# A second gate copy on the sync queue, ReLUs on two engines, and a newly searched order in a fused attention and gated FFN kernel

## The chip, the cores and the metric

The kernel runs on one core of a Trainium2 chip. The metric is the device time of one execution in microseconds (us), lower is better. The core has five engines with queues of their own: TensorE (PE, with its weight loads as PEld), VectorE (DVE), ScalarE (ACT), GpSimd (POOL) and SyncE (SP, which here only starts transfers). Transfers that SP, ACT or POOL start run on 16 DMA engines.

## The reference

Forgetting attention over 8 batches of 8 heads, 576 positions and head width 64, and then a gated FFN with a convolution of three taps along the sequence. All inputs and the output are float32.

```python
q, k, v, f: (8, 8, 576, 64), f: (8, 8, 576)
scores = q @ k.T / 8
cum = cumsum(log(clip(f, 1e-4, 1)), axis=-1)
scores = where(causal, -1e9, scores + cum[:, None] - cum[None, :])
x = softmax(scores) @ v                      # heads side by side: (8, 576, 512)
h = maximum(x @ w_in, 0)                     # (8, 576, 1024)
conv = sum over k of conv_w[k] * h shifted by k - 1 along the sequence
out = (h * sigmoid(conv)) @ w_out            # (8, 576, 512)
```

## The kernel before, in words

The work is cut into named tasks. A task has the engines that it may run on, the tasks that must stand before it, and rooms that it takes and gives back: four PSUM tiles `ps` of 1024 float32 columns, six tiles `pp` for probabilities, two buffers `hg` for the FFN's hidden units and so on. The string `ORDER` is a list of all tasks; `Plan.play` runs through it once and issues each task's instructions, with the engine behind the `@` where a task has a choice. So `ORDER` sets the order on each engine, and which buffer a task gets. The engines then run their own queues and wait for one another by semaphores.

A half batch (`hb`, 16 of them) is four heads. For it:

- `q{hb}.0` and `q{hb}.1` load q and k by a transposing transfer that leaves the high and low half of each float32 in alternate rows (L229). `cl` scales these rows and sets constant ones (L235). The even rows then get the decay: `rw` writes three rows from a small DRAM image (L251, L252); from half batch 8 on, without `cl`, `fi` writes 60 rows of zeros and four rows (L243, L245). Four buffers `qk` are used in turn. For half batches 0 and 1, `ld` loads plainly, `tp` turns on PE (L215) and `cl` copies out of PSUM (L221, L223).
- `v` loads values (L258) and `va` casts them (L266, L268).
- `st`, `sd` and `so` are scores on PE (L359): the tails of 64 positions, the diagonal blocks of two heads, and the off-diagonal blocks of one head. `et`, `ed` and `eo` are their exponentials on ACT (L379, L400, L417). For half batches 0 to 7 a matmul adds the causal mask (L367); from 8 on POOL masks behind the exponential (`mt`, `md`, L382, L403).
- `pv` multiplies with the values (L441, L445), `n` normalizes on DVE (L453, L455), and `t` with `tx` turns the result on PE and copies it (L462, L472). For half batches 10 to 15 `tx` is a transposing transfer from SP instead (L467).

For a batch `b`, with eight slices `ff` of 128 hidden units: `f{b}.{ff}` is the first matmul (L481), `r` the ReLU with a factor of one half (L491), `c` and `d` the two steps of the convolution on DVE (L496, L498), `a` a tanh on ACT (L501), `g` the gate on DVE (L505), `k` a copy of the last 64 positions so that two batches share one block (L510), `o` the second matmul (L516), `e` the copy from PSUM and `s` the store. The last batch's `o`, `e` and `s` go by chunks of 128 positions and by `ff` (L526, L532).

The decay at the start: f lies on 128 partitions, all 64 heads twice, loaded by two transfers of ACT's queue. `dca` clips it (L567), `dcl` takes the logarithm (L312), `dcs` is the running sum (L316), `dck` splits it into bfloat16 parts (L319, L320), `ki` writes the image. `cw` and `cwt` turn the convolution's weights on PE and make ratios of them (L341, L344 to L351). `wi` and `wo` load the weights, `wic` and `woc` cast them (L551, L559).

SP issues nearly all transfers in one queue, and an issue waits there for what its data need, with everything behind it.

## Time and profile before

| what | value |
|---|---|
| median of three runs | 255.22 us (253.63 to 257.57) |
| profiled execution: time | 254.81 us |
| profiled execution: span | 253.1 us |
| busy PE / DVE / ACT / POOL | 230.6 / 215.3 / 209.3 / 60.2 us |
| transfers | 49.98 MB, mean 197 GB/s |

The span runs from the first to the last instruction; the time has 1.7 us more around it. Busy time is the union of an engine's instructions. A group in the profile is named by line, engine, operation, and output and input, with its count, its busy time, the mean of one instruction, and the idle time ahead of it with what ended that. Chain rows give a start, a length and an engine with its tile and line; they follow back what released each step from the end of the kernel.

### The profile page before, as it was taken

How to read it: one execution, taken by the hardware profiler on the slowest of the kernel's cores; microseconds unless marked ns; L12 is line 12 of the kernel's file. 1: busy time of each engine (PE TensorE's matmuls, PEld its weight loads, DVE VectorE, ACT ScalarE, POOL GpSimd, SP SyncE). 2: the span in 40 equal slices, each digit the busy share in tenths (PEclk: the TensorE clock that was granted, in tenths of full speed). 3: DMA queues.
4: the chain of work that ended last, by engine and by line, in shares of the span. 5: the costliest groups of instructions: out<-in, count | busy, mean ns of one | idle time of the engine just before them, and what ended most of it. 6: DMA issues, size and time to landing. Idle time of an engine off the chain costs nothing.

```text
span 253.1 us, 6392 instructions
## 1 busy us (share of the span) xinstructions
PE 230.6 (91%) x2618; PEld 146.2 (58%) x2618; DVE 215.3 (85%) x322; ACT 209.3 (83%) x285; POOL 60.2 (24%) x92
## 2 busy tenths in 40 slices
PE   0799989688999999999999999999959999999992
PEld 0687765357555766766565665665645755644440
DVE  5756064999999999999999989999949999999970
ACT  2746948799899989999899999999957999679661
POOL 8302011101407102221731145402414150000100
PEclk9979999999999999999999999999989999999999
DMA  7993999999999989999999999999998954045046
GB/s 161 326 276 76 218 223 168 233 220 243 223 247 209 218 187 222 237 233 222 194 245 206 242 194 255 213 185 275 230 179 174 198 163 88 7 128 201 6 166 208
DMA packets 121013, 49.98 MB, mean 197 GB/s; under 512 B 111010, under 2 KB 111010, under 8 KB 120984
## 3 DMA queue, kind: packets, MB, share of 16 engines
q1 hardware_dynamic: 120434, 48.41, 88.9%
q0 software_dynamic: 304, 0.73, 0.9%
q10 hardware_dynamic: 246, 0.44, 0.6%
q8 instruction: 20, 0.33, 0.5%
q14 instruction: 9, 0.07, 0.1%
HBM read 21.11 MB, written 10.17 MB: 124 GB/s over the span
## 4 chain that ended last, share of the span: by engine, by line
PE 57%; DVE 15%; DMA 13%; ACT 6%; issue 4%; SPq 2%; POOL 0%; ACTq 0%; DVEq 0%
PE ps L516 21%; PE ps L481 15%; PE ps L359 9%; PE ps L441 6%; DMA qk<-in_q_dram 5%; DVE u L496 4%; DVE u L498 3%; ACT pp L417 3%; DMA qk<-blank 3%; DVE hg L505 2%; DMA qk<-in_k_dram 2%; DMA u<-in_f_dram 2%; PE ps L445 2%; DVE xm L455 1%; PE ps L367 1%
## 5 line engine op out<-in xcount | busy, mean ns | idle before, releaser
L481 PE MATMUL ps<-xt,w_in_f 128*128 128x512 f16 (+1 forms) x512 | 69.3, 286 | 2.1 <-POOL w_in_f L559 1.6
L359 PE MATMUL ps<-qk 128*128 128x64 bf16 (+2 forms) x576 | 63.9, 242 | 4.5 <-DMA qk<-blank 2.6
L417 ACT ACTIVATE pp<-ps 128x1024 f16<-128x1024 f32 x64 | 64.0, 1042 | 2.8 <-PE ps L364 1.9
L516 PE MATMUL ps<-w_out_f,hg 128*128 128x512 f16 x256 | 59.3, 379 | 0.0
L498 DVE SCALAR_TENSOR_TENSOR u<-ht,cwt,u 128x576 f32<-128x576 f16 x64 | 56.2, 895 | 0.7
L496 DVE SCALAR_TENSOR_TENSOR u<-ht,cwt 128x576 f32<-128x576 f16 x64 | 54.0, 853 | 0.8 <-ACT ht L491 0.7
L501 ACT ACTIVATE hg<-u,cw 128x576 f16<-128x576 f32 x64 | 48.8, 788 | 5.5 <-DVE u L498 5.2
L359 PEld LDWEIGHTS <-qk 128*128 128x128 bf16 x576 | 39.8, 99 | 22.9 <-issue 4.6
L481 PEld LDWEIGHTS <-w_in_f 128*128 128x128 f16 x512 | 34.3, 98 | 31.3 <-POOL w_in_f L559 1.9
L505 DVE SCALAR_TENSOR_TENSOR hg<-hg,ht 128x576 f16<-128x576 f16 x64 | 50.2, 810 | 0.5 <-ACT hg L501 0.5
L491 ACT ACTIVATE ht<-ps 128x576 f16<-128x576 f32 x64 | 41.6, 674 | 6.3 <-DVE hg L505 2.6
L516 PEld LDWEIGHTS <-hg 128*128 128x128 f16 x256 | 23.8, 98 | 25.8 <-DVE hg L505 0.8
L403 POOL TENSOR_SCALAR_AFFINE_SELECT pp<-pd 128x1024 f16<-128x1024 f32 x16 | 20.4, 1282 | 55.8 <-ACT pd L400 55.8
L441 PE MATMUL ps<-va,pp 128*128 128x65 f16 x640 | 25.0, 196 | 1.4 <-ACT pp L417 1.2
L455 DVE TENSOR_TENSOR xm<-ps,rc 128x896 f16<-128x896 f32 (+1 forms) x32 | 24.2, 758 | 1.1
L441 PEld LDWEIGHTS <-pp 128*128 128x128 f16 x640 | 23.0, 99 | 3.7 <-ACT pp L417 1.1
L400 ACT ACTIVATE pd<-ps 128x1024 f32<-128x1024 f32 x16 | 16.4, 1041 | 5.0 <-PE ps L359 4.2
L400 ACT ACTIVATE pp<-ps 128x1024 f16<-128x1024 f32 x16 | 16.1, 1040 | 4.1 <-PE ps L359 4.1
L510 POOL COPY tl<-hg 128x512 f16<-128x512 f16 (+1 forms) x9 | 5.9, 669 | 45.6 <-DVE hg L505 45.6
L453 DVE RECIPROCAL rc<-ps 128x14 f32<-128x14 f32 (+1 forms) x32 | 6.6, 206 | 11.5 <-PE ps L441 7.7
L367 PE MATMUL ps<-mask,ident 128*128 128x512 bf16 (+1 forms) x40 | 14.7, 370 | 0.7 <-ACT pp L417 0.6
L266 POOL CAST va<-vf 128x1024 f16<-128x1024 f32 x7 | 8.5, 1226 | 25.9 <-PE ps L359 11.6
(91 smaller groups left out, 202.8 us busy)
## 6 DMA issues: line engine op xcount, KB each, us to landing
vf<-in_v_dram SPq DMA_DIRECT2D x32, 256.0 KB, 4.3
out_dram<-ob SPq DMA_DIRECT2D x14, 512.0 KB, 2.8
qk<-blank SPq DMA_DIRECT2D x8, 540.0 KB
ob<-in_moe_w_in_dram SPq DMA_DIRECT2D x4, 512.0 KB
ob<-in_moe_w_out_dram SPq DMA_DIRECT2D x4, 512.0 KB, 4.6
vf<-in_v_dram SPq DMA_DIRECT2D x8, 128.0 KB, 2.9
out_dram<-ob SPq DMA_DIRECT2D x4, 256.0 KB
out_dram<-ob SPq DMA_DIRECT2D x7, 128.0 KB, 2.8
```

The lines of the kernel that those rows point to most:

```text
L359: nc.tensor.matmul(o, tk[:, h * S + k0:h * S + k0 + 128], tq[:, h * S + q0:h * S + q0 + n], start=first, stop=last and not by_matmul(hb, h))
L400: nc.scalar.activation(o, ps_of(f"sd{i}").rearrange("p (s c) -> p s c", s=2), AF.Exp, scale=SCALE)
L417: nc.scalar.activation(pair(i)[:, s, 512:1536], ps_of(f"so{i}.{s}"), AF.Exp, scale=SCALE)
L441: nc.tensor.matmul(ps[:, c:c + D + 1], block(hb, h, m, n), va[:, h, m, 0:D + 1], start=(m == 0), stop=(m == n))
L455: nc.vector.tensor_tensor(x.rearrange("p (j h d) -> p j h d", j=a, d=D), got[:, :, :, 0:D], r.unsqueeze(3).broadcast_to((128, a, g, D)), o ...
L481: nc.tensor.matmul(ps[:, c:c + n], w_in_f16[:, cc, 128 * ff:128 * (ff + 1)], xt[:, cc // 2, x:x + n], start=(cc == 0), stop=(cc == NCC - 1))
L491: nc.scalar.activation(ht_of(b, ff)[:, 1:1 + S], ps_of(f"f{b}.{ff}")[:, 0:S], AF.Relu, scale=0.5)
L496: nc.vector.scalar_tensor_tensor(u, ht[:, 0:S], cwt[:, ff, 0:1], ht[:, 1:1 + S], op0=ALU.mult, op1=ALU.add)
L498: nc.vector.scalar_tensor_tensor(u, ht[:, 2:2 + S], cwt[:, ff, 1:2], u, op0=ALU.mult, op1=ALU.add)
L501: nc.scalar.activation(hg_of(b, ff), u_t[slot[f"c{b}.{ff}", "u"]], AF.Tanh, scale=cw[:, ff, 1:2])
L505: nc.vector.scalar_tensor_tensor(hv, hv, 1.0, ht_of(b, ff)[:, 1:1 + S], op0=ALU.add, op1=ALU.mult)
L516: nc.tensor.matmul(ps[:, 512 * (c % 2):512 * (c % 2 + 1)], w, w_out_f16[:, ff, :], start=(ff == 0), stop=(ff == NFF - 1))
```

## The change

Six things change in the code, and the order of all tasks with them.

The second copy of f is issued by SP instead of ACT. The load of the exponential's table is a task `tb` that must stand behind `dcl`, and each exponential behind `tb`. A ReLU may run on ACT or on DVE; on DVE it is a multiplication and a maximum in one instruction. A weight cast may also run on DVE. The last batch's chunk 1 is copied out in two halves of 256 columns, one on ACT and one on DVE, and stored by two transfers, of SP and of ACT. `ORDER` is another list. In it nine of the 64 ReLUs are on DVE (r0.0, r0.2, r0.6, r2.1, r3.3, r4.2, r4.5, r4.6, r6.2), DVE has four `tx` copies instead of seven and five output copies instead of four beside the half chunk, and `wic1` is on POOL, `woc3` on DVE. Chunk 1 of the last batch is the last one now instead of chunk 3. The clamp cl1.1.1, the last that rw1 needs, is on ACT behind scores of half batch 0 instead of on DVE.

On PE, st2, so5.0, so4.0 and so5.1 stood among f0.0 to f0.4; now so5.0, so4.0, so4.1, sd7, so7.1, sd6, st3 and so6.0 do. On SP, rw3 stood behind q5.1, v1.0 and v1.2, now ahead of q5.1. Around half batch 14, PE now has f4.7, so24.1, sd26, sd27, o3.2, so26.1, f5.0, so27.0, o3.3, f5.1, f5.2, f5.3, so25.0, f5.4, so27.1, so26.0, o4.0, st13, sd28, with n11.1 on DVE while f4.7 runs. Behind pv13.1 it has f5.5, f5.6, f5.7, so28.1, o3.4, f6.0, f6.1, o4.2, sd31. Behind the last gate g7.7 the list has 22 matmuls of the last batch where it had 18.

```diff
 ORDER = """
-ld0 ld0.1.1 ld0.0.0 ld0.0.1 ld0.1.0 tp0.0.0 tp0.0.1 ld1 dca dcl tp0.1.0 tp0.1.1 cl0.0.0@ACT dcs dck ki@POOL ld1.0.0
+dca dcl ld0 v0.0 ld0.0.0 ld1 tb cw cwt ld0.0.1 ld0.1.0 tp0.0.0 ld0.1.1 dcs tp0.0.1 tp0.1.0 v0.4 ld1.0.0 dck ld1.0.1
...
     nc.scalar.dma_start(fsb[0:BH], f.rearrange("b h s -> (b h) s"))
-    nc.scalar.dma_start(fsb[BH:128], f.rearrange("b h s -> (b h) s"))
+    nc.sync.dma_start(fsb[BH:128], f.rearrange("b h s -> (b h) s"))
     nc.scalar.preload_act_table(AF.Ln)
     nc.scalar.dma_start(cwrow, moe_conv_w)
...
     def decay_log():
         nc.scalar.activation(fsb, fsb, AF.Ln)
-        nc.scalar.preload_act_table(AF.Exp)
...
-    def relu(b, ff):
-        nc.scalar.activation(ht_of(b, ff)[:, 1:1 + S], ps_of(f"f{b}.{ff}")[:, 0:S], AF.Relu, scale=0.5)
+    def relu(b, ff, e):
+        o, i = ht_of(b, ff)[:, 1:1 + S], ps_of(f"f{b}.{ff}")[:, 0:S]
+        if e == "ACT":
+            nc.scalar.activation(o, i, AF.Relu, scale=0.5)
+        else:
+            nc.vector.tensor_scalar(o, i, 0.5, 0.0, op0=ALU.mult, op1=ALU.max)
...
+    def evac_half(b, c, x):
+        o = ob_t[slot[f"e{b}.{c & ~1}", "ob"]][:, c % 2, 256 * x:256 * (x + 1)]
+        i = ps_of(f"o{b}.{c & ~1}.0")[:, 512 * (c % 2) + 256 * x:512 * (c % 2) + 256 * (x + 1)]
+        (nc.vector.tensor_copy if x else nc.scalar.copy)(o, i)
+
+    def store_half(b, c, x):
+        r = b * S + 128 * c
+        (nc.scalar if x else nc.sync).dma_start(outf[r:r + 128, 256 * x:256 * (x + 1)],
+                                                ob_t[slot[f"e{b}.{c & ~1}", "ob"]][:, c % 2, 256 * x:256 * (x + 1)])
...
+    add("tb", "ACT", [], lambda: nc.scalar.preload_act_table(AF.Exp), behind=["dcl"])
...
-            add(f"{w}c{j}", "POOL/ACT", [f"{w}{j}"], lambda e, w=w, j=j: stage_cast(w, j, e), give=[("ob", f"{w}{j}")])
+            add(f"{w}c{j}", "POOL/ACT/DVE", [f"{w}{j}"], lambda e, w=w, j=j: stage_cast(w, j, e), give=[("ob", f"{w}{j}")])
...
-            add(f"r{b}.{ff}", "ACT", [f"f{b}.{ff}"], lambda b=b, ff=ff: relu(b, ff), take=["ht"], give=[("ps", f"f{b}.{ff}")])
+            add(f"r{b}.{ff}", "ACT/DVE", [f"f{b}.{ff}"], lambda e, b=b, ff=ff: relu(b, ff, e), take=["ht"], give=[("ps", f"f{b}.{ff}")])
...
         if last:
             for c in range(NKB):
+                if c == 1:
+                    for x in range(2):
+                        add(f"e{b}.{c}.{x}", ("ACT", "DVE")[x], [f"o{b}.{c}.{NFF - 1}"], lambda b=b, c=c, x=x: evac_half(b, c, x),
+                            behind=[f"e{b}.{c - 1}"])
+                        add(f"s{b}.{c}.{x}", ("SP", "ACT")[x], [f"e{b}.{c}.{x}"], lambda b=b, c=c, x=x: store_half(b, c, x))
+                    continue
```

Three places of the new order follow, each as it stands on an engine's queue before and then after the change. Line numbers of the changed kernel are its own.

DVE where the first FFN begins, before. `xt` copies are tx0 and tx1, the clamps of `qk1` and `qk3` belong to half batches 5 and 3, and `u0` from `ht0` is the first convolution.

```order
L472 COPY xt0_117<-ps3_136 128x1152
L472 COPY xt0_117<-ps2_135 128x1152
L235 TENSOR_SCALAR qk1_86<-qk1_86,lim_76 128x2304
L496 SCALAR_TENSOR_TENSOR u0_124<-ht0_119,cwt_72 128x576
L235 TENSOR_SCALAR qk3_88<-qk3_88,lim_76 128x2304
L498 SCALAR_TENSOR_TENSOR u0_124<-ht0_119,cwt_72,u0_124 128x576
```

The same place after; `ht0` from `ps2` is a ReLU on DVE.

```order
L238 TENSOR_SCALAR qk3_88<-qk3_88,lim_76 128x2304
L474 COPY xt0_117<-ps1_134 128x1152
L497 TENSOR_SCALAR ht0_119<-ps2_135 128x576
L502 SCALAR_TENSOR_TENSOR u0_124<-ht0_119,cwt_72 128x576
L238 TENSOR_SCALAR qk1_86<-qk1_86,lim_76 128x2304
L504 SCALAR_TENSOR_TENSOR u0_124<-ht0_119,cwt_72,u0_124 128x576
```

The first ReLU and the first convolution moved ahead of the clamp of half batch 5, and one xt copy left DVE.

SP where half batch 14 is loaded into `qk2`, before: the transfers of `xm` are tx10 and tx11, the blank and image rows are fi14.

```order
L229 DMA_TRANSPOSE qk2_87<-in_k_dram 128x2304
L258 DMA vf0_89<-in_v_dram 128x8x64 x2
L467 DMA_TRANSPOSE xt1_118<-xm1_110 128x9x128
L537 DMA out_0_dram<-ob0_130 128x2x512
L467 DMA_TRANSPOSE xt1_118<-xm0_109 128x9x128
L258 DMA vf0_89<-in_v_dram 64x8x64
L537 DMA out_0_dram<-ob2_132 128x2x512
L229 DMA_TRANSPOSE qk2_87<-in_q_dram 128x2304
L258 DMA vf1_90<-in_v_dram 128x8x64 x2
L243 DMA qk2_87<-blank_66 60x4x1152
L245 DMA qk2_87<-image_65 4x2x2304
```

The same place after.

```order
L469 DMA_TRANSPOSE xt1_118<-xm1_110 128x9x128
L232 DMA_TRANSPOSE qk2_87<-in_q_dram 128x2304
L469 DMA_TRANSPOSE xt1_118<-xm0_109 128x9x128
L232 DMA_TRANSPOSE qk2_87<-in_k_dram 128x2304
L261 DMA vf1_90<-in_v_dram 128x8x64 x2
L246 DMA qk2_87<-blank_66 60x4x1152
L248 DMA qk2_87<-image_65 4x2x2304
```

The two stores and the tail load of v that stood between tx10 and the second load of half batch 14 are gone from there.

SP where half batch 15 is filled, in `qk3`, before: the two transfers of `xm` are tx12 and tx13.

```order
L229 DMA_TRANSPOSE qk3_88<-in_q_dram 128x2304
L229 DMA_TRANSPOSE qk3_88<-in_k_dram 128x2304
L258 DMA vf1_90<-in_v_dram 128x8x64 x2
L243 DMA qk3_88<-blank_66 60x4x1152
L245 DMA qk3_88<-image_65 4x2x2304
L467 DMA_TRANSPOSE xt0_117<-xm1_110 128x9x128
L467 DMA_TRANSPOSE xt0_117<-xm0_109 128x9x128
```

The same place after.

```order
L232 DMA_TRANSPOSE qk3_88<-in_q_dram 128x2304
L261 DMA vf0_89<-in_v_dram 128x8x64
L469 DMA_TRANSPOSE xt0_117<-xm0_109 128x9x128
L553 DMA out_0_dram<-ob1_131 128x2x512
L261 DMA vf0_89<-in_v_dram 64x8x64
L469 DMA_TRANSPOSE xt0_117<-xm1_110 128x9x128
L246 DMA qk3_88<-blank_66 60x4x1152
L248 DMA qk3_88<-image_65 4x2x2304
```

Both transfers of `xm`, a store and a load of v now stand ahead of the fill.

110 lines of the change are left out of this document (57 added, 53 removed).

## The prediction

> **What bounds the kernel now.** I read the page first, then the busy time by stretches of the span, then the chain of waits, the waits of each engine, and the timeline at the places that the change touches. The page shows three engines near their limit.
>
> ```profile
> span 253.1 us, 6392 instructions
> PE 230.6 (91%) x2618; PEld 146.2 (58%) x2618; DVE 215.3 (85%) x322; ACT 209.3 (83%) x285; POOL 60.2 (24%) x92
> ```
>
> The next view cuts the span into stretches. In each row stand the length, then the busy time of PE, PEld, DVE, ACT and POOL, the granted TensorE clock, the DMA share and GB/s.
>
> ```profile
> 0.00:14.10 14.10, 5.93 (x63) 5.45 (x64) 9.27 (x26) 6.56 (x6) 7.20 (x34) 0.97 0.95 248
> 14.10:39.20 25.10, 24.02 (x336) 18.37 (x334) 12.39 (x22) 16.19 (x19) 2.59 (x3) 0.95 0.96 188
> 39.20:60.00 20.80, 16.46 (x190) 10.18 (x190) 16.82 (x22) 18.83 (x27) 3.10 (x4) 1.00 1.03 220
> 60.00:80.00 20.00, 19.03 (x214) 11.97 (x214) 19.23 (x28) 18.66 (x26) 5.89 (x5) 1.00 1.06 225
> 80.00:180.00 100.00, 99.38 (x1224) 63.71 (x1223) 96.99 (x139) 95.37 (x132) 29.77 (x35) 1.00 1.09 222
> 180.00:190.00 10.00, 7.36 (x99) 5.29 (x97) 6.55 (x11) 6.95 (x10) 2.74 (x3) 0.87 1.11 200
> 190.00:240.00 50.00, 50.00 (x467) 27.76 (x465) 48.95 (x71) 40.96 (x61) 8.33 (x8) 0.99 0.47 121
> 240.00:253.10 13.10, 8.40 (x39) 3.48 (x37) 5.06 (x10) 5.81 (x10) 0.59 (x3) 0.97 0.51 181
> ```
>
> PE is idle for 253.1 - 230.6 = 22.5 us: 8.2 before the first score matmul at 14.1, 1.1 to 39.2, 4.3 to 60, 1.0 to 80, 0.6 in the next hundred, 2.6 in the stretch 180:190, none to 240, and 4.7 at the end. The matmuls that remain are as dense as they get: in the last chain piece below, 64 of them take 13.83 us, 216 ns each. The change leaves the number of matmuls alone, so on PE only these 22.5 us can be won. DVE is next. From 80 to 180 it is busy 97.0%, from 190 to 240 97.9%.
>
> ```profile
> 234.58 13.83 PE ps L516 x64
> 248.43 0.58 ACT ob L526
> ```
>
> For DVE I take the stretch in which the FFN runs, from the first convolution to the last gate; the two rows behind it, of the timeline, are its two ends.
>
> ```profile
> 43.30:244.30 201.00, 192.46 (x2170) 118.41 (x2167) 192.06 (x274) 180.24 (x252) 48.80 (x51) 0.99 0.92 196
> ```
>
> ```profile
> 42.51 0.88 DVE L235 TENSOR_SCALAR qk<-qk,lim 128x2304 uint16<-128x2304 uint16 x1 [3.40 <-DMA qk<-in_q_dram]
> ...
> 242.86 1.42 DVE L505 SCALAR_TENSOR_TENSOR hg<-hg,ht 128x576 f16<-128x576 f16 x2
> ```
>
> The clamp at 42.51 (cl5.0) waits for its transposing load, and the first convolution stands behind it. The last gate ends at 244.28, and 8.8 us later the span ends. Between 42.51 and 244.28 lie 201.8 us, of which DVE works 192.06 + 0.8 = 192.9 and is idle 8.9. So PE and DVE are both within 5% of full there: what helps one alone is soon stopped by the other.
>
> **The change, part by part.**
>
> *Second half of f on SP, cwt ahead of the sum.* The decay chain starts the kernel. These are pieces of the chain, a wait of SP's queue, and rows of the timeline.
>
> ```profile
> 1.39 5.69 DMA u<-in_f_dram
> ...
> 8.39 1.37 DVE u L316
> ...
> 11.07 1.49 DVE qk L223
> ```
>
> ```profile
> SPq L258 <- DMA u<-in_f_dram: 2.2, 1, 2.2
> ```
>
> ```profile
> 5.44 0.37 SPq L258 DMA_DIRECT2D vf<-in_v_dram  x1
> ...
> 11.04 0.66 PE L341 MATMUL ps<-one,pd 3*128 3x3 f32 x8 [0.59 <-ACT qk L221]
> ...
> 13.85 0.17 DVE L344 COPY cw<-ps 128x24 f32<-128x24 f32 x1
> ...
> 15.00 0.16 DVE L351 TENSOR_TENSOR cwt<-cw,cwt 128x8 f32<-128x8 f32 x1
> ```
>
> The second copy is issued at 1.39 and lands at 7.08; SP's load at 5.44 was released by the first, so that one had landed. Issued first on SP, the second should land by 5.44 too: 1.6 us earlier. But DVE now makes the conv ratios before the running sum, and PE their transposes before all else. The conv row takes the place in ACT's queue that the second f copy leaves, so I put its landing between 5.4 and 7.1; then come 0.66 us on PE and 15.16 - 13.85 = 1.3 on DVE, and the sum starts between 7.4 and 9.1 instead of 8.39. What is won on f is mostly spent again; ratios no longer lie between the clamps later. Bounds for the first FFN matmul: 2.0 earlier to 1.3 later (when rw1's last clamp, now on ACT behind scores, comes late by that). I take **-0.6**. The exp table as a task of its own has one answer: it stands behind dcl on ACT as before, 0. SP's loads of q and k stand behind one more issue and v0.0; they are covered, since their clamps wait for the decay rows until 11.07.
>
> *More scores ahead of f0.4.* PE's waits have one for the third weight cast.
>
> ```profile
> PE ps L481 <- POOL w_in_f L559: 1.6, 1, 1.6
> ```
>
> In the changed order two more diagonal and two more off-diagonal blocks of scores stand between f0.0 and f0.4, and rw3, on which they rest, is issued before q5.1 instead of behind it. Bounds -1.6 to 0. I take **-1.0**, nearer to the row than to 0, because the added scores need rw3's landing, which this trace can't show.
>
> *The stall at 184.* The chain shows it, with the length of a score block and of an f in its first two rows; the rows behind are of the timeline.
>
> ```profile
> 130.71 0.44 PE ps L359 x4
> 131.14 0.98 PE ps L481 x8
> ...
> 173.98 5.88 DMA qk<-in_q_dram
> ...
> 179.87 6.46 DMA qk<-blank
> ...
> 186.43 1.04 PE ps L359 x12
> ```
>
> ```profile
> 170.82 1.66 SPq L467 DMA_TRANSPOSE xt<-xm  x1
> ...
> 174.15 3.10 PE L481 MATMUL ps<-xt,w_in_f 128*128 128x512 f16 x24
> ...
> 193.84 0.95 SPq L243 DMA_DIRECT2D qk<-blank  x1
> ...
> 200.31 1.06 PE L359 MATMUL ps<-qk 128*128 128x128 bf16 x16
> ```
>
> fi14 is issued 9.0 us after tx11, because q14.0 stands behind tx11, a v load that waits for GpSimd, and a store. Behind the change only q14.1 and two loads stand between: 1.5 + 5.9 = 7.4 us, landing 6.5 later, 13.9 us after tx11. In the changed order PE has, from n11.1's end, the rest of f4.7, four score blocks and o3.2, 0.2 + 1.8 + 1.7 = 3.7 us, until f5.0, and then 10.2 until sd28 (five f at 0.98, o3.3 and o4.0 at 8 x 0.216 = 1.73, four score blocks at 0.44, a tail): it arrives at 13.9. The wait of 2.6 goes. So does the slow clock behind it: 0.13 of 10 us in the row 180:190 and up to 0.01 of 50 in the next, 1.3 to 1.8 us. Bounds -4.4 to 0, taken **-4.1** on PE. The Trainium skill, page "TensorE: Matmul & The Clock Gate", section "Part 1: The HAM clock gate (the "warmup" mystery)", says that the clock falls after an idle window of about 3.4 us. By that rule a wait of 2.6 us would leave the clock alone, and this term would be -2.6. The trace disagrees, since the clock fell behind this wait; so I keep the larger value.
>
> *fi15 behind tx12 and tx13.* Before, fi15 went out at 193.84 and was used at 200.31, 6.5 us later, without a wait. Now both transposes of xm, a store and a v load stand ahead of it on SP, and tx13 waits for n13.1. PE has 2.9 + 0.4 + 1.7 = 5.1 us of work between pv13.1 and f6.0, and 3.7 more to sd31. tx12 and tx13 take 1.3 to 3 us each to issue, with 1.2 between; landing within 3.3 us, as tx11 to f5.0 above. That makes 0 to 3.6 us of new waiting, **+1.5** taken.
>
> *Work that changes engines.* Rows of the groups, by form:
>
> ```profile
> L491 ACT ACTIVATE ht<-ps 128x576 f16<-128x576 f32 x64 | 41.6, 674 | 6.3 <-DVE hg L505 2.6 <-PE ps L481 2.5 <-ACT hg L501 0.8
> ...
> L472 DVE COPY xt<-ps 128x1152 f16<-128x1152 f16 x7 | 5.1, 751 | 1.0 <-PE ps L464 1.0
> ...
> L268 POOL CAST va<-vf 64x256 f16<-64x256 f32 x6 | 3.1, 522 | 16.3 <-DMA vf<-in_v_dram 16.3
> ...
> L522 DVE COPY ob<-ps 128x1024 f32<-128x1024 f32 x2 | 2.4, 1219 | 0.3 <-PE ps L516 0.3
> ...
> L526 DVE COPY ob<-ps 128x512 f32<-128x512 f32 x1 | 0.7, 692 | 0.8 <-PE ps L516 0.8
> ```
>
> A ReLU on DVE has no row. From PSUM, 512 columns take 692 ns and 1024 take 1219, 1.03 ns a column; 576 take 0.76 us (bounds 0.69 and 0.85, the latter the convolution's mean in the page). Nine move. ACT loses 9 x 0.674 = 6.1 us; it was not the last to come free, so that wins nothing by itself. On DVE, within the stretch from cl5.0 to the last gate: 8 x 0.76 = +6.1 (r0.0 and c0.0 now run ahead of cl5.0, in the 3.40 us for which DVE waited there: -0.8 for c0.0); two xt copies fewer, -1.5; one v cast fewer and one weight cast more, 0; two output copies of 1024 more and one of 512 fewer, +1.8. Less 0.6 for the overlap of neighbours (two convolutions show 1.54, not 1.62): **+5.0 us of DVE work**, 197.9 in all. The other weight cast moves from ACT to GpSimd, at 33 us, where both wait for data: 0.
>
> *Last chunk in halves.* A copy of 256 columns takes 0.43 us on DVE by the same slope, against 0.58 for the last copy on ACT: **-0.15**. The stores carry the same bytes; I count nothing there (bounds -0.5 to +0.3, two issues beside each other on two queues).
>
> **The sum.** PE's side: -0.6 - 1.0 - 4.1 + 1.5 - 0.2 = -4.4, a span of 248.7. DVE's side: start of cl5.0 at 42.5 - 0.6 = 41.9; 197.9 of work; idle 2.0, that is 99% busy, between the 97.9% of 190:240 and full, because the stall (10 - 6.55 of the row 180:190) goes; the last gate then ends at 241.8. Behind it stand 22 matmuls instead of 18, +0.9, less 0.15: 8.8 + 0.7 = 9.5 to the end. That is a span of 251.3. The later side decides: 251.3, or 1.8 less than before. The profiled execution took 254.81, 1.7 beside its span; so **253.0**. The median of the three runs is 255.22, 0.4 over the profiled one, and I leave that difference out.
>
> **The rivals.** *PE's side decides* (0.25): DVE's added work fits into waits that its row counts as busy. For it speaks that ACT gets 6 us freer, so that PSUM buffers come back sooner. It gives 248.7 + 1.7 = 250.4, and 248.5 where the start wins its full 2.0 and the w_in wait its 1.6.
>
> *DVE runs no fuller than from 80 to 180* (0.2): at 97%, 197.9 takes 204.0, the last gate ends at 245.9, and the time is 255.4 + 1.7 = 257.1, slower than before. It decides from a DVE share under 98.1%, where 41.9 + 201.7 + 9.5 is the old span. Against it: from 80 to 180 PE was busy 99.4%, so DVE's 3% there were mostly waits for PE, and from 190 to 240 it stood at 97.9%, next to that point. For it stands a stretched convolution, 1.70 us instead of 0.82, while a GpSimd mask of 1.10 runs:
>
> ```profile
> 171.91 1.10 POOL L403 TENSOR_SCALAR_AFFINE_SELECT pp<-pd 128x1024 f16<-128x1024 f32 x1 [8.86 <-ACT pd L400]
> 171.92 1.70 DVE L498 SCALAR_TENSOR_TENSOR u<-ht,cwt,u 128x576 f32<-128x576 f16 x1
> ```
>
> Three more v tails move to GpSimd, 3 x 0.52 us, worth 0.8 each us beside such a convolution: +1.3. The Trainium skill, "GPSIMD Engine Reference", section "1. Specifications", states this as a rule against moving work there: the SBUF interfaces are shared, and DVE instructions with two SBUF inputs contend. The two rows above bear it out.
>
> *The wait moves to fi15* (0.1): 3.6 us, and the clock falls as above, 1.5: PE's side is 248.7 + 3.6 = 252.3, 254.0 in time.
>
> *The new order does nothing* (0.05): every wait reappears, 253.1 + 1.7 = 254.8. The forecast itself has 0.4; its own range is 251 to 255.
>
> **How the numbers follow.** The range 247.5 to 257.5 reaches from PE's side with its best terms to the DVE rival; outside it I leave the full sum of all gains and the case of several late costs, 2 in 10. Two per cent of 255.2 is 5.1 us, about what a measurement of this kernel can tell from no change. Faster than 250.1: most of PE's side and a little of the forecast, 0.27. Slower than 260.3: the tail of the DVE rival and of fi15, 0.10. Within: 0.63.
>
> **What would show it.** f landing by 5.5 and the running sum between 7.4 and 9.1; no PE wait for a qk<-blank transfer near 184 and the clock at 1.00 there; PE waiting at most 3 us for xt or qk<-blank just before the last scores; DVE at 98 to 99% between its first convolution and the last gate, with nine ReLUs near 0.76; the end 9 to 10 us behind the last gate. The forecast is wrong if PE's idle time falls by over 6 us with DVE under 97%, or if DVE's own work grows by clearly more than 5.

## The result, and the profile after

The changed kernel takes 255.94 us in the median of 20 executions (254.53 to 261.17); the kernel before, run beside it, 256.35 in the median of 20 (252.62 to 259.49). The ratio of the two, taken over the executions that lie within 1.5% of the fastest of their kernel, is 1.0103 with a 95% interval of 1.0071 to 1.0134: about one per cent slower, where 0.7% faster had been forecast, and less than the two per cent from which a kernel is called faster or slower here. The two medians are nearly equal all the same, because only 10 of the 20 executions of the kernel before are as quick as those that the ratio is taken from, and 15 of the 20 of the changed one. The profiled execution of the changed kernel took 255.84 us, its span 254.1; the forecast was 253.0 and the profiled one of before 254.81. So the gain of 1.8 us did not come; the time is inside the range of 247.5 to 257.5.

The page's busy times, and the stretches of the prediction for the changed kernel (columns as there):

```profile
span 254.1 us, 6397 instructions
...
PE 229.6 (90%) x2618; PEld 144.8 (57%) x2618; DVE 218.6 (86%) x328; ACT 205.5 (81%) x276; POOL 65.3 (26%) x96
```

```profile
0.00:14.10 14.10, 6.08 (x58) 5.33 (x59) 10.63 (x32) 4.56 (x4) 7.40 (x34) 1.00 0.89 247
14.10:39.20 25.10, 23.62 (x349) 18.22 (x347) 10.87 (x15) 18.99 (x22) 5.08 (x5) 1.00 1.15 202
39.20:60.00 20.80, 17.66 (x207) 11.15 (x206) 18.39 (x24) 19.39 (x28) 2.51 (x3) 1.00 1.02 213
60.00:80.00 20.00, 18.10 (x213) 11.68 (x211) 19.56 (x29) 18.14 (x25) 7.77 (x10) 1.00 1.02 225
80.00:180.00 100.00, 98.17 (x1184) 62.40 (x1183) 97.62 (x137) 91.66 (x123) 28.88 (x30) 1.00 1.07 218
180.00:190.00 10.00, 8.76 (x156) 6.43 (x155) 8.98 (x13) 8.63 (x13) 4.43 (x6) 1.00 1.08 257
190.00:240.00 50.00, 46.91 (x422) 25.19 (x423) 45.66 (x71) 38.16 (x57) 6.38 (x9) 0.97 0.43 115
240.00:254.10 14.10, 10.28 (x48) 4.38 (x45) 6.90 (x13) 5.91 (x10) 2.82 (x2) 1.00 0.48 168
```

PE's idle time is the first number less the second. It was 8.2, 1.1, 4.3, 1.0, 0.6, 2.6, 0 and 4.7 us; now it is 8.0, 1.5, 3.1, 1.9, 1.8, 1.2, 3.1 and 3.8, in all 24.5 instead of 22.5. What the stretches 39.2:60 and 180:190 and the two ends gained (3.6 together) is lost again at 14.1:39.2, at 60 to 180 and above all at 190:240, where before there was no idle time (5.6 together). Two shorter stretches of it, and waits that are new, four of PE and one of ACT behind which PE waits in its turn:

```profile
190.00:200.00 10.00, 6.91 (x67) 3.68 (x68) 9.90 (x18) 7.55 (x12) 0.38 (x2) 1.00 1.05 240
200.00:210.00 10.00, 10.00 (x116) 5.85 (x114) 6.02 (x9) 6.75 (x10) 1.86 (x3) 0.83 0.04 9
```

```profile
PE ps L483 <- DMA xt<-xm: 4.2, 2, 3.1
...
PE ps L464 <- DVE xm L457: 1.4, 2, 1.2
...
ACT ob L528 <- DMA out_dram<-ob: 1.4, 1, 1.4
...
PE ps L443 <- ACT ob L528: 1.2, 1, 1.2
...
PE ps L483 <- DVE xm L457: 1.0, 1, 1.0
```

The timeline of PE and of SP's queue shows the place. `L469` are tx12 and tx13, `L553` the store s4.0, `L261` value loads, and the 12 matmuls of `L483` f6.0 and f6.1:

```profile
186.35 2.40 PE L443 MATMUL ps<-va,pp 128*128 128x65 f16 x72 [1.24 <-ACT ob L528]
...
195.47 0.65 PE L483 MATMUL ps<-xt,w_in_f 128*128 128x512 f16 x4
199.22 2.18 PE L483 MATMUL ps<-xt,w_in_f 128*128 128x512 f16 x12 [3.09 <-DMA xt<-xm]
201.21 3.04 PE L522 MATMUL ps<-w_out_f,hg 128*128 128x512 f16 x8
```

```profile
185.64 4.21 SPq L232 DMA_TRANSPOSE qk<-in_q_dram  x1
189.89 0.58 SPq L261 DMA_DIRECT2D vf<-in_v_dram  x1
190.87 2.14 SPq L469 DMA_TRANSPOSE xt<-xm  x1
193.11 0.52 SPq L553 DMA_DIRECT2D out_dram<-ob  x1
193.72 0.69 SPq L261 DMA_DIRECT2D vf<-in_v_dram  x1
194.51 1.73 SPq L469 DMA_TRANSPOSE xt<-xm  x1
```

tx12 waits behind q15.0 and v7.2, tx13 behind s4.0 and v7.4. PE has the first four matmuls of f6.0 from tx12, then waits 3.1 us for tx13. Behind that the clock is 0.83 in the mean of 200:210, so eight matmuls of 512 columns take 3.04 us instead of the 1.89 that eight of the same line take at 205, and DVE is busy for only 6.0 of these 10 us. The wait for fi14 that stood at 184 is gone, and the clock in 180:190 is 1.00.

### The profile page after: what moved, and what is told of

Read it like the earlier page. It is cut to its first block, busy times and chain, and to the rows that moved or that the text cites. A ratio compares the mean times of both kernels' runs of the same rounds, so it can differ in the third digit from the quotient of the medians.

```text
span 254.1 us, 6397 instructions
## 1 busy us (share of the span) xinstructions
PE 229.6 (90%) x2618; PEld 144.8 (57%) x2618; DVE 218.6 (86%) x328; ACT 205.5 (81%) x276; POOL 65.3 (26%) x96
## 2 busy tenths in 40 slices
DMA packets 121157, 49.98 MB, mean 197 GB/s; under 512 B 111026, under 2 KB 111282, under 8 KB 121128
## 4 chain that ended last, share of the span: by engine, by line
PE 59%; DMA 19%; SPq 7%; ACT 7%; DVE 5%; issue 2%; ACTq 0%
PE ps L522 19%; PE ps L483 18%; PE ps L361 10%; DMA qk<-in_k_dram 7%; PE ps L443 5%; SPq L232 4%; DMA hg<-in_q_dram 3%; ACT pp L419 3%; DMA qk<-blank 3%; PE ps L369 2%; DMA out_dram<-ob 2%; DMA xt<-xm 2%; DMA qk<-image 2%; PE ps L447 2%; DVE u L502 1%
## 5 line engine op out<-in xcount | busy, mean ns | idle before, releaser
L483 PE MATMUL ps<-xt,w_in_f 128*128 128x512 f16 (+1 forms) x512 | 70.1, 288 | 5.6 <-DMA xt<-xm 4.2
L419 ACT ACTIVATE pp<-ps 128x1024 f16<-128x1024 f32 x64 | 64.8, 1033 | 7.1 <-PE ps L361 6.7
L361 PE MATMUL ps<-qk 128*128 128x128 bf16 (+2 forms) x576 | 62.2, 240 | 1.8 <-ACT ht L495 0.8
L522 PE MATMUL ps<-w_out_f,hg 128*128 128x512 f16 x256 | 60.9, 384 | 0.0
L504 DVE SCALAR_TENSOR_TENSOR u<-ht,cwt,u 128x576 f32<-128x576 f16 x64 | 53.5, 846 | 0.8
L483 PEld LDWEIGHTS <-w_in_f 128*128 128x128 f16 x512 | 34.5, 98 | 34.4 <-issue 6.5
L361 PEld LDWEIGHTS <-qk 128*128 128x128 bf16 x576 | 38.9, 98 | 20.3 <-issue 2.2
L495 ACT ACTIVATE ht<-ps 128x576 f16<-128x576 f32 x55 | 35.5, 663 | 6.3 <-PE ps L483 5.6
L443 PE MATMUL ps<-va,pp 128*128 128x65 f16 x640 | 23.8, 193 | 2.4 <-ACT ob L528 1.2
L457 DVE TENSOR_TENSOR xm<-ps,rc 128x896 f16<-128x896 f32 (+1 forms) x32 | 24.3, 758 | 1.1
L402 ACT ACTIVATE pp<-ps 128x1024 f16<-128x1024 f32 x16 | 16.5, 1030 | 7.4 <-PE ps L366 5.8
L516 POOL COPY tl<-hg 128x512 f16<-128x512 f16 (+1 forms) x9 | 9.6, 1069 | 40.6 <-DVE hg L511 40.6
L238 DVE TENSOR_SCALAR qk<-qk,lim 128x2304 uint16<-128x2304 uint16 x12 | 11.7, 979 | 6.5 <-DMA qk<-in_q_dram 5.4
L384 POOL TENSOR_SCALAR_AFFINE_SELECT pt<-p 128x256 f16<-128x256 f32 x8 | 4.8, 604 | 43.5 <-ACT p L381 43.5
```

What stands on the lines that cost most here:

```text
L361: nc.tensor.matmul(o, tk[:, h * S + k0:h * S + k0 + 128], tq[:, h * S + q0:h * S + q0 + n], start=first, stop=last and not by_matmul(hb, h))
L402: nc.scalar.activation(o, ps_of(f"sd{i}").rearrange("p (s c) -> p s c", s=2), AF.Exp, scale=SCALE)
L419: nc.scalar.activation(pair(i)[:, s, 512:1536], ps_of(f"so{i}.{s}"), AF.Exp, scale=SCALE)
L443: nc.tensor.matmul(ps[:, c:c + D + 1], block(hb, h, m, n), va[:, h, m, 0:D + 1], start=(m == 0), stop=(m == n))
L457: nc.vector.tensor_tensor(x.rearrange("p (j h d) -> p j h d", j=a, d=D), got[:, :, :, 0:D], r.unsqueeze(3).broadcast_to((128, a, g, D)), o ...
L483: nc.tensor.matmul(ps[:, c:c + n], w_in_f16[:, cc, 128 * ff:128 * (ff + 1)], xt[:, cc // 2, x:x + n], start=(cc == 0), stop=(cc == NCC - 1))
```

## The experiments

The kernel before was run beside every group of experiments: its medians there were 256.59, 256.13, 255.48, 255.88 and 255.41. Times are medians of all executions with their number, ratios are to the kernel before with the 95% interval. Views are of one execution each; where that one is far from its median, the text says so. The theory to begin with: the new list loses at the end of SP's queue what it wins at fi14. The rivals: DVE decides; and the transfers decide, whatever their order.

### Single parts undone

f's second half back on ACT's queue.

```diff
-    nc.sync.dma_start(fsb[BH:128], f.rearrange("b h s -> (b h) s"))
+    nc.scalar.dma_start(fsb[BH:128], f.rearrange("b h s -> (b h) s"))
```

> The changed kernel with the second half of f on ACT's queue again, behind the first. Theory 'the load of half batch 1 decides the start': PE's first score waits for the turns of half batch 1, whose load lands at 13.1; f comes about 1.5 us later, the running sum starts at 8.5 instead of 7.0, and the decay rows are still done before 13.1, so the first score moves by less than 0.5 us and the time by nothing, ratio 1.010. SP's loads go out one issue earlier, which may win 0.5. Rival 'the decay chain decides the start': the first score comes 1.5 us later and the time grows by 1.0 to 1.5 us, ratio 1.015.

Measured: 260.19 (6), 1.018 [0.9993, 1.0368]. The start of the changed kernel first, then of this one: clipping, running sum, first mask matmul.

```profile
4.63 0.58 DVE L583 TENSOR_SCALAR u<-u 128x576 f32<-128x576 f32 x1 [0.27 <-DMA u<-in_f_dram]
...
6.97 1.35 DVE L318 TENSOR_TENSOR_SCAN u<-one,u 128x576 f32<-128x576 f32 x1
...
13.17 0.68 PE L218 MATMUL ps<-ident_b,hg 128*128 128x128 bf16 x9 [1.05 <-DMA hg<-in_q_dram]
...
13.68 0.38 PE L369 MATMUL ps<-mask,ident 128*128 128x512 bf16 x1
```

```profile
6.85 0.46 DVE L583 TENSOR_SCALAR u<-u 128x576 f32<-128x576 f32 x1 [2.49 <-DMA u<-in_f_dram]
...
7.68 0.98 PE L343 MATMUL ps<-one,pd 3*128 3x3 f32 x8 [7.68 <-DMA pd<-in_moe_conv_w_dram]
...
9.94 1.35 DVE L318 TENSOR_TENSOR_SCAN u<-one,u 128x576 f32<-128x576 f32 x1
...
15.53 0.38 PE L369 MATMUL ps<-mask,ident 128*128 128x512 bf16 x1 [0.72 <-DVE qk L226]
```

In the new list the copy on SP is worth 1.85 us at the first score, more than either theory said; the profiled execution of this run is a long one, though, 263.57 us, and some of the 1.85 may be its own. The reason is not f alone: the conv row, third on ACT's queue, now lands later too (PE's matmuls on it start at 7.68 instead of 4.71), and the ratios stand ahead of the sum on DVE, which starts 3.0 us later. Against the kernel before (first mask matmul at 13.98) the changed one wins only 0.3, since in the changed one half batch 1's load decides. The median moves by 4 us over six executions; how much of that is the start's, the scatter doesn't let one say.

The last chunk whole again, and all ReLUs on ACT:

```diff
-                if c == 1:
+                if False:
-o7.1.7 e7.1.0 e7.1.1 s7.1.1 s7.1.0
+o7.1.7 e7.1@ACT s7.1
```

> The changed kernel with its last chunk copied whole by ACT and stored by one transfer of SP, as the other chunks are. Reading of the two ends: from PE's last matmul to the span's end the kernel before takes 4.7 us (copy 0.58, store and landing 4.1), the changed one 3.8 (two copies one behind the other, 0.37 and 0.42, and 2.9 from the last store's issue). If the smaller store is what shortens the end, this is 0.9 us slower than the changed kernel, ratio 1.014. If the difference lies in what else is under way, or the halves gain nothing since they run one behind the other, it is equal within 0.3 us, ratio 1.010.

```diff
-r0.0@DVE r0.2@DVE r0.6@DVE r2.1@DVE r3.3@DVE r4.2@DVE r4.5@DVE r4.6@DVE r6.2@DVE
+r0.0@ACT r0.2@ACT r0.6@ACT r2.1@ACT r3.3@ACT r4.2@ACT r4.5@ACT r4.6@ACT r6.2@ACT
```

> The changed kernel with all 64 ReLUs on ACT, in the places that the list gives them. Theory 'order of SP': DVE loses 6.8 us of work that mostly lies beside PE's own, ACT has 205 of 254 us busy and takes 9 x 0.65 = 5.9 us more; the waits for xt stay, so within 1 us of the changed kernel, ratio 1.005 to 1.013. Rival 'DVE decides': the last gate comes up to 6.8 us earlier, 2 to 5 us won, ratio 0.99 to 1.00. Rival 'ACT decides': ACT's exponentials come later behind the ReLUs, 2 to 4 us lost, ratio 1.02.

Measured: 256.56 (12), 1.0076 [1.0004, 1.0148] for the whole chunk and 257.41 (6), 1.0113 [0.9956, 1.0271] for the ReLUs: neither can be told from the changed kernel. The two ends, with halves and whole:

```profile
250.32 0.37 ACT L537 COPY ob<-ps 128x256 f32<-128x256 f32 x1 [1.10 <-PE ps L522]
250.72 0.34 SPq L541 DMA_DIRECT2D out_dram<-ob  x1
250.72 0.42 DVE L537 COPY ob<-ps 128x256 f32<-128x256 f32 x1 [3.50 <-ACT ob L537]
251.18 0.39 ACTq L541 DMA_DIRECT2D out_dram<-ob  x1
```

```profile
250.31 0.59 ACT L532 COPY ob<-ps 128x512 f32<-128x512 f32 x1 [1.10 <-PE ps L522]
250.93 0.34 SPq L548 DMA_DIRECT2D out_dram<-ob  x1
```

From the first copy to the span's end it is 254.1 - 250.32 = 3.8 us with halves and 254.2 - 250.31 = 3.9 whole. The halves win 0.1; they run one behind the other, DVE waiting for ACT's.

The code of the change with the old list:

```diff
 the list of before, with
+tb behind dcl; every ReLU @ACT
-e7.3@ACT s7.3
+e7.3.0 e7.3.1 s7.3.1 s7.3.0
-                if c == 1:
+                if c == 3:
```

> The code of the change with the list of before: f's second half on SP, the table load as a task behind dcl, the last chunk (chunk 3 here) in halves; all ReLUs on ACT. Reading of the two ends and starts: the halves win 0.9 us at the end, f lands 1.6 us earlier and the running sum, not the load of half batch 1, sets the start here, so 0.5 to 1.5 more: together 1 to 2 us, ratio 0.992 to 0.996. Rival 'the parts win nothing': what they give at the start is lost again at the waits for transfers in the middle, and the end is set by other things, ratio 1.00.

Measured: 255.80 (6), 1.0116 [1.0033, 1.0198]; its median is 0.3 under that of before. Its profile has the wait for fi14 still (2.5 us) and a first mask matmul at 13.71. The parts alone win nothing that can be seen; that is the rival. Their ratio is as far above 1 as that of the changed kernel, with a median below that of before: six executions do not settle whether the parts cost something.

### Repairs of single places

Four moves in the new list. Only the tasks of the two engines concerned are shown.

```diff
 SP
-fi14 q15.1 s2.1 v7.0
+fi14 s2.1 q15.1 v7.0
-tx12 s4.0 v7.4 tx13 fi15
+tx12 tx13 fi15 s4.0 v7.4
 PE
-so28.1 o3.4 f6.0 f6.1 o4.2 sd31 so31.1 o4.3
+so28.1 o3.4 o4.2 o4.3 f6.0 f6.1 sd31 so31.1
```

> The changed kernel with four moves in its list and nothing else: tx13 stands directly behind tx12 on SP (the store s4.0 and the value load v7.4 go behind it), fi15 directly behind tx13, the store s2.1 ahead of the load q15.1, and o4.2 and o4.3 ahead of f6.0 on PE. Theory 'order of SP near the end': the changed kernel loses 3.1 us in PE's wait for xt at 199, 1.2 us in the wait for e4.0 behind the store at 186, and about 1.7 us by the slow clock from 200 to 210; with the moves these go, less about 1 us that is left, so 4 to 5 us less than the changed kernel, a ratio to the kernel before of 0.99. Rival 'DVE decides': DVE works 195 of the 205 us between its first convolution and last gate, so PE's gain is taken back by waits for DVE and at most 1.5 us is won, ratio 1.005 or more. Rival 'bytes decide': the transfers run without a gap until 200 whatever their order, so tx13 and fi15 land where they did and the PE wait only moves, ratio 1.01.

Measured: 255.47 (12), 1.0025 [0.9949, 1.0101], half a microsecond under the changed kernel in the median and 0.8% in the ratio; the intervals overlap, and the 4 to 5 us of the theory did not come. The profiled execution (257.5 us of span, 3.8 us over the median in time) has no wait for xt near 200 any more, but this at 144, and a clock of 0.83 from 140 to 150. `sd22` waits there for fi11's rows: they were issued at 136.6, and in the changed kernel such rows are used 7.3 us after their issue. The gate that the second row names was done at 142.0, two microseconds too early to be what ended the wait; the weight load of the same matmuls, in the first row, names the rows. In the changed kernel's profile the same wait is 0.71.

```profile
144.07 0.53 PEld L361 LDWEIGHTS <-qk 128*128 128x128 bf16 x8 [3.33 <-DMA qk<-blank]
144.08 0.79 PE L361 MATMUL ps<-qk 128*128 128x128 bf16 x8 [3.02 <-DVE hg L511]
```

The next run goes for that place, and a third adds the ReLUs:

```diff
 SP
-s1.2 s0.1 v6.0 fi11 v5.0
+fi11 s1.2 v6.0 s0.1 v5.0
```

> The four moves of the run a_fix, and the stores s0.1 and s1.2 and the value load v6.0 behind fi11 on SP instead of ahead of it. In the profiled run of a_fix PE waits 3.0 us at 144 for the blank rows of fi11, which land 7.3 us after their issue behind those stores, and the clock falls behind it; in the changed kernel's profile the same wait is 0.7. Theory 'a load behind stores': the rows land about 2 us earlier, the wait and the slow clock at 140 to 150 go in most executions, and the time falls by 1 to 3 us against a_fix, ratio 0.99 to 0.995. Rival 'the wait only moves': the stores then delay the loads that follow, q12.1 and v5.0, and the time is that of a_fix, 1.00.

> The changed kernel with the four moves of the run a_fix and with all ReLUs on ACT, all stores in place. Theory 'two limits': a_fix took the waits for transfers at 190 to 200 down and gained 0.5 us in the median, since DVE came next; with 6.8 us less on DVE as well both go, 252 to 254, ratio 0.985 to 0.995. Rival 'only transfers decide': the ReLUs make no difference as in the run a_relu_act, 255 to 256, ratio 1.00.

Measured: 259.27 (6), 1.0196 [1.0092, 1.0300] for the stores behind fi11, a clear loss: e2.0 takes the buffer that s1.2 gives back, so it now has to wait for that store, and PE waits for the tile that e2.0 holds.

```profile
ACT ob L528 <- DMA out_dram<-ob: 3.9, 1, 3.9
PE ps L443 <- ACT ob L528: 3.5, 1, 3.5
```

With ReLUs on ACT instead: 255.46 (12), 1.0034 [0.9991, 1.0076], the same as a_fix. Its profile shows no wait for xt near 200, but 2.1 us for blank rows at 142 and 2.8 for xm at 60.

The mirror image in the old list, its stall at 184 taken away:

```diff
 SP
-tx11 v6.4 s1.1 q14.0 v7.0 v7.1 fi14
+tx11 v6.4 q14.0 s1.1 fi14 v7.0 v7.1
```

> The kernel before with three transfers of SP moved and nothing else: the load q14.0 ahead of the store s1.1 instead of behind it, and the value loads v7.0 and v7.1 behind fi14 instead of ahead of it. Theory 'a load behind stores': q14.0 goes out 0.7 us earlier and lands without 512 KB ahead of it (2.3 us at 220 GB/s), and fi14's rows land about 3 us earlier; the wait of 2.6 us at 184 and the slow clock behind it (1.5) go, 2 to 4 us less than before, ratio 0.985 to 0.992. Rival 'the wait only moves': what is put behind fi14 delays q15.0 and q15.1 and the wait comes back at fi15, ratio 1.00.

Measured: 256.29 (12; 253.23 to 260.48), 1.0033 [0.9977, 1.0089]. In the profile (252.0 us of span) the wait at 184 and the slow clock are gone, and the span is 1.1 us shorter, not 4.1: three other waits of PE have grown by 3.8 us together, at 60 (for a cast of v, from 1.0 to 1.9), at 97 (for an output copy, 1.4) and at 199 (for a convolution, 1.5). The mechanism works, and the median stays where it was. So the one wait that the profile of before showed was not the gain that I took it for. That other executions lose elsewhere fits this, but only one of each kernel has a profile.

### Without the stores of batches 0 to 4

```diff
     def store(ev, b, c):
         ob, r = ob_t[slot[ev, "ob"]], b * S + 128 * c
+        if b < 5:
+            return
```

> The changed kernel without the output stores of batches 0 to 4 (12 stores, 5.6 MB of the 50 MB; that part of the output isn't written). The rest of the work is the same. Theory 'transfers decide': the transfers run without a gap until 200 us, and PE's waits late in the middle are waits for them; 5.6 MB at the 210 GB/s of that stretch are 26 us of transfer time, so the waits for xt (4.2), for the store behind e4.0 (1.2), for blank rows (0.7) and the slow clock (1.7) go: 5 to 7 us less than the changed kernel, ratio 0.985 to 0.99. Rival 'DVE decides': DVE works 195 of 205 us in the FFN's stretch, so no more than 2 us is won, ratio 1.00 or more.

> The kernel before without the output stores of batches 0 to 4, as in the run beside it. Theory 'transfers decide': its wait for fi14 at 184 (2.6), the slow clock behind it (1.5) and the loads that DVE waits for at 39 (3.4, not all of it on PE) go: 4 to 5 us less, ratio 0.980 to 0.985, and the changed kernel without stores is within 1 us of this one or faster: the new list lost by where its stores and loads stand. Rival 'DVE decides': with transfers out of the way this is faster than the changed kernel without stores by 2 us or more, since DVE has 3.3 us more work there.

By the pages' totals the stores are 5.8 MB (49.98 against 44.20). Measured: new list 253.76 (11; 251.86 to 256.23), 1.0025 [0.9972, 1.0079]; old list 249.35 (5; 248.97 to 250.53), 0.9860 [0.9787, 0.9934]. The stores, with what waits for them, cost the old list some 6.8 us and, as far as five executions show, most of its scatter (they lie within 1.6 us, 20 executions of the whole kernel within 6.9); they cost the new list 2.2. With them out of the way the new list is 4.4 us behind. This speaks against the theory that it lost only by where stores and loads stand, and looked like DVE. Two runs test DVE's ReLUs:

> The changed kernel without the output stores of batches 0 to 4 (that part of the output isn't written) and with all ReLUs on ACT. Without stores the changed kernel takes 253.8 us and the one before 249.4; from the first convolution to the last gate DVE is 96.5% busy in the one (194.6 of 201.7) and 97.1% in the other (191.4 of 197.1). Theory 'DVE decides once transfers don't': 6.0 us of DVE work less at the same share takes 6 us off that stretch, until PE decides: 3 to 6 us less than without stores alone, 248 to 251. Rival 'the list decides': the order on PE and ACT lost the 4.4 us, not DVE's work, so this stays within 1 us of 253.8; and if ACT comes late with 5.9 us more, it is slower.

```diff
 the list of before, without those stores, and
-r0.0 r0.2 r0.6 r2.1 r3.3 r4.2 r4.5 r4.6 r6.2
+r0.0@DVE r0.2@DVE r0.6@DVE r2.1@DVE r3.3@DVE r4.2@DVE r4.5@DVE r4.6@DVE r6.2@DVE
```

> The kernel before without the output stores of batches 0 to 4, with the nine ReLUs on DVE that the change puts there (r0.0, r0.2, r0.6, r2.1, r3.3, r4.2, r4.5, r4.6, r6.2), in the old list's places. Theory 'DVE decides once transfers don't': 9 x 0.75 = 6.8 us more of DVE work at 97% makes it 4 to 7 us slower than the 249.4 of this kernel without the move, 253 to 256. Rival 'the list decides': DVE has room beside PE, so within 1.5 us of 249.4.

Measured: 253.49 (11) for the new list with its ReLUs on ACT, no change; 260.76 (5), 1.0221 [1.0154, 1.0287] for the old list with nine on DVE, 11 us more. Neither is what "DVE decides" said. In the old list r0.6 stands behind convolutions, gates and a cast on DVE, and PE waits for the PSUM tile that it reads; the clock is 0.66 in the mean of 50:60. This wait and another of 2.0 us for a ReLU on DVE are a part of the 11 us; the rest was not taken apart.

```profile
54.35 0.59 PE L370 MATMUL ps<-mask,ident 128*128 128x512 bf16 x1 [4.38 <-DVE ht L498]
```

So ReLUs on DVE cost by their place in its queue, and in the new list's places they cost nothing that can be seen. It is the rest of the list that loses the 4.4 us.

### The two lists joined

The first tasks of one list, then all that is left in the order of the other; the join is at about 97 us.

```diff
+ORDER = first(new, up to so15.0) + [x for x in old if x not in it]     # h_newold
+ORDER = first(old, up to the same place) + [x for x in new if x not in it]     # h_oldnew
```

> The new list up to so15.0 of half batch 7 (about 97 us), and behind it what is left in the order of the old list; without the output stores of batches 0 to 4 (not written). Known beside it: new list 253.8, old list 249.4. Theory 'the second part loses': PE's waits of the new list from 170 to 210 (2.9 us without stores) are gone, so 250 to 251. Rival 'the first part loses' (waits and a slow clock at 50 to 70): 253 or more.

> The old list up to the same place, and behind it the rest in the order of the new list; without the output stores of batches 0 to 4 (not written). Theory 'the second part loses': 252 to 253.5. Rival 'the first part loses': 249 to 250.

Measured without those stores: new then old 250.41 (5), 0.9817 [0.9754, 0.9879]; old then new 254.60 (11), 0.9965 [0.9922, 1.0009]. The second part loses 3.3 us or more; the first part is equal within about 1 us (1.1 worse in one pair, 0.8 better in the other). Both joined kernels have the code of the change, so the code alone doesn't lose the 4.4 us either.

> The new list up to so15.0 (with the f load on SP and the nine ReLUs as far as they lie in it), the old list behind, all stores. Theory 'the second part loses': the waits at 195 to 200 of the new list go, but the old list's wait for fi14 at 184 comes back; the new first part saves what it saved at 40 to 60 (1.4 us): 1 us under the kernel before, ratio 0.995. Rival 'the first part loses': 1 to 2 us slower than before, 1.005.

> The old list up to that place (with the f load on SP), the new list behind, all stores. Theory 'the second part loses': as the changed kernel, 1.005 to 1.012. Rival 'the first part loses': 0.99.

Measured with all stores: 257.82 (12), 1.0096 [1.0053, 1.0139] and 258.94 (12), 1.0125 [1.0073, 1.0177]. By their medians both are 1.9 to 3 us slower than either list as a whole, which no theory had; by their ratios they can't be told from the changed kernel. In the profile of the first, the wait at 184 that was expected back is 0.3, but PE waits 2.9 us for image rows at 124, not far behind the join. The second, in its profile (its longest execution, 261.14 us), has the changed kernel's wait again, in the same place:

```profile
203.54 3.04 PE L483 MATMUL ps<-xt,w_in_f 128*128 128x512 f16 x12 [3.46 <-DMA xt<-xm]
```

Two last runs, again without those stores: the old order from q14.0 on (about 168 us), and the four moves of a_fix.

```diff
+ORDER = first(new, up to so24.1) + [x for x in old if x not in it]     # h2_ns
```

> The new list up to r4.7 and so24.1 (about 168 us), what is left behind it in the order of the old list; without the output stores of batches 0 to 4 (not written). Theory 'the loss lies from 168 to 205': as with the join at 97 us (250.4), 250 to 251.5. Rival 'it is spread over 97 to 165': 252.5 or more.

> The changed kernel with the four moves of the run a_fix (tx13 and fi15 directly behind tx12 on SP, the store s2.1 ahead of q15.1, which does nothing here, o4.2 and o4.3 ahead of f6.0), without the output stores of batches 0 to 4 (not written). Theory 'xt and fi15 are late': the 0.9 us at 198 to 202 go and what follows them, 252 to 253. If the wait for xm at 191, which the moves leave, decides, 253.8 as without them.

Measured: 251.16 (5), 0.9855 [0.9820, 0.9890] and 253.83 (11), 0.9965 [0.9924, 1.0005]. Of the 4.4 us, 2.6 lie behind 168 us, and not in the places that a_fix repairs. From 168 to the last gate the views of four runs without stores read, in this order: new list; new list with ReLUs on ACT; new list to 168 and then old; old list.

```profile
168.00:244.08 76.08, 73.03 (x703) 41.16 (x701) 75.25 (x107) 62.14 (x88) 18.46 (x18) 1.00 0.52 112
```

```profile
168.00:243.16 75.16, 73.40 (x724) 41.54 (x724) 74.53 (x106) 63.41 (x91) 18.24 (x18) 1.00 0.56 114
```

```profile
168.00:241.38 73.38, 72.06 (x693) 40.37 (x691) 71.48 (x103) 63.73 (x93) 13.12 (x13) 1.00 0.58 116
```

```profile
168.00:239.47 71.47, 71.32 (x692) 40.02 (x688) 70.18 (x101) 62.50 (x93) 14.01 (x14) 1.00 0.51 112
```

DVE, the third busy time, fills 98.9, 99.2, 97.4 and 98.2% of the stretch, PE 96.0, 97.7, 98.2 and 99.8%. So in the new list DVE is the fuller of the two here, and in the joined and the old one PE is; from 80 to 168 PE is fuller in the new list too, 99.6 against 97.6%. DVE has 75.25 us of work left behind 168 in the new list and 71.48 in the joined one. The groups of DVE in that stretch of the new list which the joined one lacks, or has fewer of (there the first row is x1, 0.7 us, and the others are absent):

```profile
L269 DVE CAST va<-vf 128x1024 f16<-128x1024 f32 x3 | 2.3, 756 | 0.0
...
L528 DVE COPY ob<-ps 128x1024 f32<-128x1024 f32 x1 | 1.2, 1209 | 0.0
...
L497 DVE TENSOR_SCALAR ht<-ps 128x576 f16<-128x576 f32 x1 | 0.8, 756 | 0.0
```

Two casts, one output copy and one ReLU are 1.6 + 1.2 + 0.8 = 3.6 us. A normalization more (L457, x5 against x4) is another 1.1, and what the joined list has more of takes about 1 away again, so the whole difference is 3.8, beside one in the last gate of 2.7 (244.08 against 241.38). And of the nine ReLUs only r6.2 lies here; eight lie where PE is the fuller engine, which fits that moving all nine did nothing. In that run DVE has 0.7 us less behind 168 and the last gate comes 0.9 earlier, but its median moves by only 0.3, which the scatter hides. The joined list changes the order of all engines behind 168 us, though; these 3.6 us were not moved by themselves, so that they are the cause is not shown.

No version with all its stores beats the kernel before: a_fix, a_fix_relu and b_fi14 are nearest to it, and their ratios include 1.

## Why the prediction was wrong

The forecast went by DVE's side of the sum: cl5.0 at 41.9, 197.9 us of work, 2.0 idle, and 9.5 from the last gate to the end. The same four read 41.3, 194.3, 10.0 and 8.5 in the changed kernel:

```profile
41.32:245.61 204.29, 193.08 (x2180) 118.11 (x2178) 194.28 (x277) 178.16 (x244) 52.69 (x57) 0.99 0.88 192
```

The step that failed is the idle time, 2.0 against 10.0; the other three came out smaller than forecast. DVE was idle for 8.9 us before, of which the stretch of the stall holds 3.45 (10 - 6.55). The other 5.4 were all but left out as well, with no row that says why they should go. The argument nearest to one, that DVE's 3% from 80 to 180 were mostly waits for PE, is not in the trace: of the 3.0 us idle there it waits 0.9 for PE and 1.0 for ACT. With the 5.4 left in, the sum is 41.9 + 197.9 + 5.4 + 9.5 + 1.7 = 256.4, slower than before: the gain that was forecast came out of this term. Of the 10.0, 4.0 lie in 200:210, behind PE's wait for xt, and 4.6 ahead of 168, where it was 4.1 before. The terms one by one:

*f on SP, cwt ahead of the sum* (-0.6, bounds -2.0 to +1.3). f had landed by 4.6 rather than 5.4, and the sum began at 6.97, ahead of the 7.4 to 9.1 given, since the conv row was there by 4.7. The first score won 0.3 only, because the load of half batch 1 lands at 13.1, which the prediction had called covered. The first FFN matmul, for which the bounds were, came at 38.41 instead of 39.16, 0.75 earlier: right, though the first score gives less than half of it.

*More scores ahead of f0.4* (-1.0). The wait for the weight cast went, as said. PE's idle time between 39.2 and 80 fell from 5.3 to 5.0 us, no more: at 58 and 63 stand new waits for xm (1.0 and 1.2), which I had not asked for.

*The stall at 184* (-4.1). It went, with its slow clock, but to take it whole for a gain of the kernel was wrong. b_fi14 takes the same wait out of the old list: 3.8 us come back in other places, and the median stays. Without the stores that list falls to 249.35 and five executions lie within 1.6 us. So most of the scatter seems to come from the stores, and the wait at 184 may have been one draw of it; no second profile of the kernel before shows that.

*fi15 behind tx12 and tx13* (+1.5, bounds 0 to 3.6): the term of PE's side that was mis-sized most. I had looked at fi15; the one that came late was tx13 itself, 3.1 us, and the clock fell behind it, 0.17 of the ten microseconds 200:210, 1.7 us. Two more of the same kind were not in the sum: 1.1 us for xt behind tx11 at 171 (the other of the two waits in the row 4.2, 2, 3.1), and 1.2 for e4.0, whose buffer the store s2.1 still read, since s2.1 now stands behind q15.1. Together 7.1 against 1.5, and the 5.6 between them are more than the 4.4 that PE's side was to win. a_fix shows that moves can take the xt wait away; that this gives the time back it doesn't show.

*DVE's side* (197.9 us of work at 99%, last gate at 241.8). The price of a ReLU was right: 754 ns against 0.76. The work and the share were not. From the first convolution to the last gate, the stretch that was to show 98 to 99%, DVE worked 195.05 us of 205.06, 95.1%, and the last gate ended at 245.6:

```profile
40.55:245.61 205.06, 193.85 (x2186) 118.63 (x2185) 195.05 (x277) 178.93 (x245) 52.69 (x57) 0.99 0.89 193
```

The second convolution step, which I had let stand or grow beside GpSimd, became shorter, 846 ns in the mean instead of 895, although GpSimd had more to do (65.3 against 60.2 us). Over 64 of them that is 3.1 of the 3.6 us of work that were forecast too much:

```profile
L498 DVE SCALAR_TENSOR_TENSOR u<-ht,cwt,u 128x576 f32<-128x576 f16 x64 | 56.2, 895 | 0.7
```

```profile
L504 DVE SCALAR_TENSOR_TENSOR u<-ht,cwt,u 128x576 f32<-128x576 f16 x64 | 53.5, 846 | 0.8
```

So the price of +1.3 for the shared interfaces did not show here, neither in my row of a stretched convolution nor by the rule of the Trainium skill ("GPSIMD Engine Reference", "1. Specifications") that I had put beside it; what shortened the mean wasn't tried. A second error is to spread DVE's work evenly over 200 us. In the new list without the stores DVE is the fullest engine only behind 168 us. There 3.8 us more of its work go with a last gate 2.7 us later, while ahead of it 6 us of ReLUs count for nothing that can be seen. With all stores DVE is idle for 5.4 of the 77.6 us between 168 and the last gate, 3.1 of them in the wait that follows PE's wait for xt: there the transfers come first, and DVE next. The prediction took a sum over the kernel where, by these runs, one over the last third was wanted.

*Last chunk in halves* (-0.15): 0.1 measured. The end came 8.5 us behind the last gate, 9.5 forecast; where that microsecond comes from was not tried.

*The rivals.* "The wait moves to fi15" (0.1, 254.0) came nearest in kind: a wait moves some microseconds along SP's queue, with the clock behind it. "DVE no fuller than 97%" is what came of the share: 95.1 in all, and 194.3 of 200.3 us or 97.0 without the 4.0 us that follow the wait for xt. Its time of 257.1 was too long only because DVE's work was smaller and the end shorter. "PE's side decides" was wrong by the terms above: PE's idle time grew by 2.0 us where that side had it fall.

What stays open: why joined lists with all stores have higher medians than both of their parents; whether DVE's late work is what the last part of the new list loses by; how the first part of the new list stands to the old one within 1 us; and what the repaired new list would give with its late casts back on ACT or GpSimd.
